# The last three token tiles as a block of two and a block of one, with the second column half's rows put off

## The chip, the cores and the metric

One core of a Trainium2 chip runs the whole program. The metric is the device time of one execution in microseconds (us). The core has TensorE (PE; PEld is its weight load), VectorE (DVE), ScalarE (ACT), GpSimd (POOL) and SyncE (SP), whose queue starts every DMA here.

## The reference

Three layers in a row over 4608 tokens of width 512; the heads' outputs of the first are one token's x.

```python
# attention in chunks of 64 tokens, 8 batches x 8 heads, head size 64
attn = softmax(q_c @ k_c.T / 8);  out = attn @ v_c
# feed-forward, hidden width 2048
g = relu(x @ w_in) ** 2;  x = g @ w_out
# soft MoE: 8 experts x 4 slots, hidden width 1024
logits = x @ phi                              # 4608 x 32
d = softmax(logits over tokens);  slot_input = d.T @ x
slot_out[e] = relu(slot_input[e] @ w1[e]) @ w2[e]
c = softmax(logits over slots);   result = c @ slot_out
```

## The kernel before

The 36 token tiles (128 tokens each) go in blocks of 1, 2, 3, 3, ... tiles, 13 blocks. A block takes 16 steps, one for each 128 of the 2048 hidden units (index f). In a step `moe_h` makes 12 matmuls with the block's x as the moving operand (3 x 128 columns for three tiles) into the PSUM tile hps; ACT applies relu (`moe_relu`) and square (`moe_square`), and two steps later (`LAG`) PE turns the result (`moe_turn`, tile gT) and `moe_keep` copies it into one of seven buffers G, a buffer for every four steps (a quad). After each quad `moe_logits` adds g times w_out times phi to the logits L. x is never multiplied with w_out in full: `soft(b)` folds each block into a running softmax over tokens (Ls, the matmul misc<-Ls,sel, exp, dd) and adds dd times G into a PSUM tile y (L933, 4 quads x tiles matmuls), which DVE adds to `acc`. Only the four G buffers of a block hold what y still needs.

`soft` is a generator: one piece in each step that follows its block. In the last block nothing follows, so its pieces stand one behind the other: L, Ls, softmax, y, acc, then `slot_turn`, `slot_rows_of` (acc times w_out, whose eight buffers are called wo) and `slot_inputs`. What comes out is siT, the input of the experts.

The expert stage reads 33.55 MB of weights: 32 units of w1 and 32 units of w2, each 512 KB (128 partitions x 1024 f32, 4 KB a partition). They have no buffers of their own. `load_units` takes the next unit in a fixed order as soon as two halves (512 f32 each) are free, and starts a DMA on SP's queue: one if the halves lie side by side (L1004), two if not (L1008). `give` at fixed steps puts buffers on that free list: those of attention when the last tiles are done with them, idle G buffers, the input weights wi after their last use (two steps each), x, and after y the last G and wo buffers. In the expert stage a unit's halves are given back as its matmuls are done. SP takes its instructions in order, so a unit that waits for a buffer holds what is behind it.

The expert stage: `ehps` (siT times w1, two groups of four experts), relu, hT by transposes, and `sop` (hT times w2 rows) into two PSUM tiles, one for each half of the 512 columns (ch 0 and 1). Of group 1 the last `FT - SPLIT` row tiles come as units `part`, one for each column half, with rows of 1 KB, so that ch 0 is done first. Then `slot_rows`, `slot_parts` (tile s) and `out_group`: the combine weights cT (made by `c_group`: four transposes and copies for four token tiles) times s, copied from PSUM by ACT and DVE in turn, and stored (9.44 MB in all, 15 stores of 512 KB, 6 of 256 KB). Five output groups of ch 0 alone go ahead, then groups of both halves, then ch 1 of the first five.

On PE the order of the main loop is the order in which the code is written; the other engines' and SP's order is a list scheduler's until the last block's `soft`, from which on ACT and DVE too go as written. `first_use[b]` is the step at which block b starts; attention of its tiles is placed 16 steps and more ahead of that. Before, the last block starts at step u0 = 152.

Of the kernel before, what the change touches and what calls it, by code (L numbers as in the profile page):

```python
# [8 lines left out]
F32 = mybir.dt.float32  # L9
# [7 lines left out]
ALU = mybir.AluOpType  # L17
# [16 lines left out]
C_CHAIN = 0  # L34
C_EARLY = 3
# [39 lines left out]
def kernel(  # L75
# [29 lines left out]
    for n in [1, 2] + [3] * ((NT - 3) // 3):  # L105
        blocks.append((t0, n))
        t0 += n
    if t0 < NT:
        blocks.append((t0, NT - t0))
    NB = len(blocks)  # L110
    bank0 = {1: 1}

    group = {b: b for b in range(NB)}
    blocks.append((0, 3))
    group[NB] = 1

# [18 lines left out]
    run_m = const.tile([P, 1], F32, name="run_m")  # L135
# [234 lines left out]
    def attention(i):  # L370
# [4 lines left out]
        xb = xb_b[max(b, 1) % 2][:, :, :, bank0.get(b, 0) * P :]  # L375
# [191 lines left out]
    def attention32(i):  # L567
# [5 lines left out]
        xb = xb_b[max(b, 1) % 2][:, :, :, bank0.get(b, 0) * P :]  # L573
# [146 lines left out]
    def moe_h(b, f):  # L720
        n = blocks[b][1] * P
        xb = xb_b[max(group[b], 1) % 2][:, :, :, cols(b)]
# [40 lines left out]
    def moe_keep(b, f, eng="act"):  # L763
        k = max(group[b], 1), f // QF
        if k not in G_q:
            G_q[k] = big.tile([P, 3, QF * P], F32, tag=f"G{n_G[0] % NG_RING}", name="G")
            n_G[0] += 1
        o0, n, c = bank0.get(b, 0), blocks[b][1], f % QF * P
        copy(eng, G_q[k][:, o0 : o0 + n, c : c + P], gt_ps.pop((b, f)))
# [18 lines left out]
    def prepare_final():  # L788

        home_ = big.tile([P, 1536], F32, tag=f"xb{NB % 2}", name="siT")  # L790
# [46 lines left out]
    def c_two(x):  # L837

        old, new = (range(max(0, 2 * y), min(C_CHAIN, 2 * y + 2)) for y in (x - 1, x))
        for g in old:  # L840
            c_parts(g, pool)
            if g + 2 < C_CHAIN:
                c_prepare(g + 2)
        for g in new:
            c_transpose(g, ps_h.tile([P, 512], F32, tag="h", name="cps"))
            c_todo.pop(0)
# [3 lines left out]
    def soft(b):  # L850
        s0, n = blocks[NB if b == 1 else b]
        last = s0 + n == NT
        if last:
# [26 lines left out]
        dve.tensor_tensor(out=rm, in0=rm, in1=run_m, op=ALU.max)  # L880
        dve.tensor_scalar_mul(nm, rm, -1.0)
# [3 lines left out]
        act.activation(out=al, in_=run_m, func=ACTF.Exp, bias=nm)  # L885
        if not last:
            dve.tensor_copy(run_m, rm)
# [29 lines left out]
        if not last:  # L917
            slots_softmax(misc()[:, : n * NS])
            yield
# [38 lines left out]
    total_G = NQ * (NB - 1)  # L958
    last_G = [x % NG_RING for x in range(total_G - NQ, total_G)]
# [3 lines left out]
    SPLIT = FT // 4  # L963
# [139 lines left out]
    pool.memset(run_m, -1e30)  # L1103
# [286 lines left out]
    at(u0 - 7, lambda: after_attention(1 - pl))  # L1390
# [5 lines left out]
    at(u0 + 9, lambda: give(*[(big, f"G{x}", 1536) for x in idle_G]))  # L1396
# [7 lines left out]
    while t < end or any(x >= t for x in slots):  # L1404
# [5 lines left out]
        if b is not None:  # L1410
# [3 lines left out]
            if (b, f) == (NB - 1, NF - 1):  # L1414
                give((big, f"xb{b % 2}", 1536))
# [173 lines left out]

    for g in range(2):  # L1590
        for ft in range(SPLIT if g else FT):
            m, t = divmod(ft, 2)
            for ch in range(NCH):
                rows_times(
                    g, ft, ch,
                    lambda ei: part_of(("rows", 4 * g + ei, m), t)[:, ch * DH : (ch + 1) * DH],
                )
            if t:
                for ei in range(4):
                    release(("rows", 4 * g + ei, m), 0)  # L1600
                    release(("rows", 4 * g + ei, m), 1)
                load_units()
# [13 lines left out]
    slot_parts(0, slot_rows(0, sops[0]))  # L1616
    firsts = [quads[0][:2], quads[0][2:], *quads[1:]]
    for ft in range(SPLIT, FT):
        if FT - ft < len(firsts):
            out_group(firsts.pop(0), (0,))  # L1620
        last_rows(1, ft)
# [38 lines left out]
```

## Time and profile before

| | |
|---|---|
| time, median of 3 runs | 762.2 us (761.36 to 765.82) |
| profiled execution: its time, its span | 762.14 us, 760.3 us |
| busy in the span | PE 93%, ACT 60%, PEld 60%, DVE 57%, POOL 21% |
| chain that ended last | PE 72%, DVE 10%, DMA 10%, ACT 2% |
| DMA | 110.48 MB; HBM read 78.71 MB, written 9.44 MB |

Busy shares are means over stages that have different limits, so the stages are read apart: the stretches of 40 slices, the windows and the chain.

### The profile page before, as it was taken

To read this page: it belongs to the slowest core of one execution; us is meant where nothing else is said; L and a number is where in the kernel's file an instruction comes from. 1 tells how busy PE (TensorE), PEld (TensorE's weight loads), DVE (VectorE), ACT (ScalarE), POOL (GpSimd) and SP (SyncE) were. 2 spreads that over 40 slices of the span, in tenths; PEclk is the share of its full clock that TensorE was granted. 3 is DMA by queue.
4 is the path that set the end of the run, shared out by engine and by line. 5 is a ranking of instruction groups with operands and counts; after the bars stand their busy time and mean duration, and the time that the engine had idled before them with its cause. 6 is when DMAs were issued, how large, how long until landed. Compare 5 with 4: busy or idle time off the path is not lost.

```text
span 760.3 us, 16721 instructions
## 1 busy us (share of the span) xinstructions
PE 704.4 (93%) x6644; PEld 455.8 (60%) x6644; DVE 430.2 (57%) x912; ACT 455.0 (60%) x947; POOL 157.2 (21%) x205
## 2 busy tenths in 40 slices
PE   5688999988999999999999999999999999979990
PEld 4577776655656566665665666656656666534550
DVE  4789996367756655566666565566655501012241
ACT  3678887664666666566566666666666555521251
POOL 3223211131222303222232122230322300000100
PEclk9899999999999999999999999999999999999996
DMA  8898834234545455434645455545546832659999
GB/s 157 220 232 214 215 120 139 65 76 84 99 93 122 94 97 97 85 84 92 123 94 107 75 99 105 105 89 105 98 84 126 227 107 84 209 184 393 364 328 322
DMA packets 233359, 110.48 MB, mean 145 GB/s; under 512 B 201537, under 2 KB 219969, under 8 KB 233281
## 3 DMA queue, kind: packets, MB, share of 16 engines
q1 hardware_dynamic: 233280, 109.41, 57.8%
q8 instruction: 53, 0.87, 0.5%
q14 instruction: 26, 0.20, 0.1%
HBM read 78.71 MB, written 9.44 MB: 116 GB/s over the span
## 4 chain that ended last, share of the span: by engine, by line
PE 72%; DVE 10%; DMA 10%; ACT 2%; POOL 1%; issue 1%; SPq 1%; DVEq 0%; POOLq 0%; ACTq 0%
PE hps L727 42%; PE gT L761 7%; PE L L778 4%; PE misc L933 4%; DMA qkT<-qk 2%; PE ehps L1477 2%; DMA unit<-in_moe_w_dram 2%; DVE qk L276 2%; DMA qkv<-in_k_dram 1%; DMA qkv<-in_v_dram 1%; PE sop L1584 1%; DMA pT<-p 1%; DVE o L1546 1%; PE misc L498 1%; DVE qk L275 1%
## 5 line engine op out<-in xcount | busy, mean ns | idle before, releaser
L727 PE MATMUL hps<-xb,wi 128*128 128x384 f16 (+2 forms) x2400 | 407.3, 320 | 0.2
L727 PEld LDWEIGHTS <-wi 128*128 128x128 f16 x2400 | 224.6, 98 | 138.2 <-issue 16.8
L742 ACT ACTIVATE g<-hps,inv_w 128x384 f32<-128x384 f32 (+1 forms) x200 | 112.6, 563 | 111.1 <-PE hps L727 109.1
L182 DVE TENSOR_REDUCE am<-qkv 128x1 bf16<-128x512 f32 x90 | 61.8, 687 | 91.3 <-DMA qkv<-in_v_dram 46.4
L188 ACT ACTIVATE G<-gT 128x384 f32<-128x384 f32 (+1 forms) x200 | 94.1, 471 | 16.9 <-PE gT L761 14.4
L761 PE MATMUL gT<-ident,g 128*128 128x128 f32 x576 | 97.7, 277 | 4.5 <-ACT G L188 3.6
L749 ACT ACTIVATE g<-g 128x384 f32<-128x384 f32 (+2 forms) x188 | 96.8, 515 | 1.5
L761 PEld LDWEIGHTS gT<-ident,g 128*128 128x128 f32 x576 | 72.8, 144 | 29.4 <-ACT g L749 6.9
L420 POOL TENSOR_SCALAR vbd<-qkv,as 64x512 f16<-64x512 f32 x54 | 37.2, 689 | 87.0 <-PE misc L500 71.4
L471 POOL TENSOR_TENSOR ex<-ex,rs 128x512 f32<-128x512 f32 x27 | 29.3, 1083 | 123.2 <-DVE rs L468 117.1
L410 DVE SCALAR_TENSOR_TENSOR qk<-qkv,as,qk 128x512 f16<-128x512 f32 x54 | 39.4, 757 | 22.1 <-ACT qk L405 21.5
L425 DVE SCALAR_TENSOR_TENSOR vbd<-qkv,as,vbd 64x512 f16<-64x512 f32 x54 | 44.5, 824 | 0.7
L778 PE MATMUL L<-g,wp 128*32 128x384 f32 x384 | 41.7, 498 | 0.0
L405 ACT ACTIVATE qk<-qkv,as 128x512 f16<-128x512 f32 x54 | 36.8, 716 | 7.2 <-DVE as L215 7.2
L484 POOL TENSOR_TENSOR p<-ex,p 128x512 f16<-128x512 f32 x27 | 36.2, 1340 | 16.8 <-ACT p L481 16.2
L481 ACT ACTIVATE p<-ex 128x512 f16<-128x512 f32 x27 | 17.0, 629 | 37.1 <-POOL ex L471 37.1
L933 PE MATMUL misc<-G,dd 128*32 128x512 f32 x288 | 35.1, 622 | 0.4 <-DVE rs__8934 L941 0.4
L435 DVE COPY qbd<-qkT 64x1024 f16<-64x1024 f16 x54 | 23.4, 433 | 18.6 <-DMA qkT<-qk 18.0
L510 DVE SCALAR_TENSOR_TENSOR xb<-misc,xb 128x512 f16<-128x512 f32 x27 | 18.5, 684 | 26.5 <-ACT xb L504 26.2
L223 POOL TENSOR_SCALAR iv_all<-ai 128x1 f32<-128x1 f32 x27 | 7.4, 274 | 106.9 <-DVE ai L218 105.9
L461 ACT ACTIVATE ex<-ex,es 128x512 f32<-128x512 f32 x27 | 19.4, 718 | 16.6 <-DVE ex L455 16.5
L859 DVE TENSOR_TENSOR Ls<-L,iv_all 128x384 f32<-128x384 f32 x12 | 6.6, 552 | 39.5 <-PE L L778 39.5
(154 smaller groups left out, 1006.0 us busy)
## 6 DMA issues: line engine op xcount, KB each, us to landing
unit<-in_moe_w_dram SPq DMA_DIRECT2D x38, 512.0 KB, 4.6
unit<-in_moe_w_dram SPq DMA_DIRECT2D x52, 256.0 KB, 5.8
qkv<-in_q_dram SPq DMA_DIRECT2D x72, 128.0 KB, 3.2
qkv<-in_k_dram SPq DMA_DIRECT2D x72, 128.0 KB, 3.5
qkv<-in_v_dram SPq DMA_DIRECT2D x72, 128.0 KB, 3.3
stage<-in_moe_w_in_dram SPq DMA_DIRECT2D x16, 512.0 KB, 5.5
stage<-in_moe_w_out_dram SPq DMA_DIRECT2D x16, 512.0 KB, 6.7
out_dram<-o SPq DMA_DIRECT2D x15, 512.0 KB, 5.5
```

Source lines behind the costliest of these rows:

```text
L182: dve.tensor_reduce(out=am, in_=src, axis=AX.X, op=ALU.max, apply_absolute_value=True)
L188: act.activation(out=out, in_=in_, func=ACTF.Copy)
L405: act.activation(out=qk16[:, 2 * a], in_=flat[:, a], func=ACTF.Copy, scale=v["s"][:, a : a + 1])
L410: dve.scalar_tensor_tensor(out=qk16[:, 2 * a + 1], in0=flat[:, a], scalar=v["s"][:, a : a + 1], in1=qk16[:, 2 * a], op0=ALU.mult, op1=ALU. ...
L420: pool.tensor_scalar(out=dst[0], in0=vin, scalar1=v["s"][pr, 2:3], scalar2=1.0, op0=ALU.mult, op1=ALU.mult,)
L425: dve.scalar_tensor_tensor(out=dst[1], in0=vin, scalar=v["s"][pr, 2:3], in1=dst[0], op0=ALU.mult, op1=ALU.subtract,)
L727: pe.matmul(hp, wi[f][:, wl, kt], xb[:, xl, kt], start=(nm == 0), stop=(nm == 3 * KT - 1))
L742: act.activation(out=g, in_=hp, func=ACTF.Relu, scale=sc)
L749: act.activation(out=g, in_=g, func=ACTF.Square)
L761: pe.transpose(gt_ps[b, f][:, j], g[:, j * P : (j + 1) * P], ident)
L778: pe.matmul(L_ps[g0][NS * x : NS * x + NS, :n], wp[:, QF * q + x], g[:, x, :n], start=(q == 0), stop=(q == NQ - 1), tile_position=(0, NS * x),
L933: pe.matmul(y[NS * g : NS * g + NS], dd[:, j], G_q[b, g][:, j], start=(j == 0), stop=(j == n - 1), tile_position=(0, NS * g), skip_group_c ...
```

## The change

The last three tiles become a block of two (b = 12) and a block of one (b = 13), 14 blocks in all. Block 12 runs in steps 152 to 167, block 13 in steps 168 to 183, and u0 is now 168. The two share one x buffer (`x_of`: tile 35 stands behind tiles 33 and 34). Block 13's quads 0, 1 and 2 are copied into the three thirds of one buffer G (quad 3 has a buffer of its own), and all these copies are made by DVE. `soft(12)` runs beside block 13's steps; its slots softmax comes behind its y.

Buffers are given at other steps. `used_G`, the four G buffers of block 12, are free after y of block 12 (step 176) instead of after the last y. Two of the c transposes and copies (`C_CHAIN`) go into the last block's chain. In the running softmax the negative maximum is kept, which makes of two DVE operations one. In the expert stage 4 row tiles of group 1 instead of 6 come as `part` units (`SPLIT`), and of group 0's row tiles 4 to 7 and group 1's 0 to 3 the ch 1 half is put off (`later`) until ch 0 is done, with output groups between.

```diff
-C_CHAIN = 0
-C_EARLY = 3
+C_CHAIN = 2
+C_EARLY = 5
...
-    for n in [1, 2] + [3] * ((NT - 3) // 3):
+    assert NT % 3 == 0
+    for n in [1, 2] + [3] * (NT // 3 - 2) + [2, 1]:
         blocks.append((t0, n))
         t0 += n
-    if t0 < NT:
-        blocks.append((t0, NT - t0))
     NB = len(blocks)
     bank0 = {1: 1}
+    x_of = {b: (max(b, 1) % 2, bank0.get(b, 0)) for b in range(NB)}
+    x_of[NB - 1] = x_of[NB - 2][0], blocks[NB - 2][1]
...
+        xb = xb_b[x_of[b][0]][:, :, :, o0 : o0 + n]
...
+            if b == NB - 1 and 0 < f // QF < 3:
+                G_q[k] = G_q[b, 0][:, f // QF : f // QF + 1]
+            else:
+                G_q[k] = big.tile([P, 3, QF * P], F32, tag=f"G{n_G[0] % NG_RING}", name="G")
+                n_G[0] += 1
...
-            c_parts(g, pool)
+            c_parts(g, dve)
...
-        dve.tensor_tensor(out=rm, in0=rm, in1=run_m, op=ALU.max)
-        dve.tensor_scalar_mul(nm, rm, -1.0)
+        dve.scalar_tensor_tensor(
+            out=nm, in0=rm, scalar=-1.0, in1=run_n, op0=ALU.mult, op1=ALU.min
+        )
...
+        if short:
+            yield
+        elif not last:
...
+        if short:
+            yield
+            slots_softmax(misc()[:, : n * NS])
...
-    total_G = NQ * (NB - 1)
-    last_G = [x % NG_RING for x in range(total_G - NQ, total_G)]
+    total_G = NQ * (NB - 2)
+    last_G = [x % NG_RING for x in range(total_G, total_G + 2)]
+    used_G = [x % NG_RING for x in range(total_G - NQ, total_G)]
...
-    SPLIT = FT // 4
+    SPLIT = FT // 2
...
-    at(u0 - 7, lambda: after_attention(1 - pl))
+    at(u0 - 12, lambda: after_attention(1 - pl))
...
-    at(u0 + 9, lambda: give(*[(big, f"G{x}", 1536) for x in idle_G]))
+    at(u0 - 5, lambda: give(*[(big, f"G{x}", 1536) for x in idle_G if x not in used_G]))
+    at(u0 + 10, lambda: give(*[(big, f"G{x}", 1536) for x in used_G]))
...
-            moe_keep(b, f)
+            moe_keep(b, f, "dve" if b == NB - 1 else "act")
...
+            now = g == 0 and ft < FT // 2
+            row_tile(g, ft, 0)
+            if now:
+                row_tile(g, ft, 1)
+                if ft % 2:
+                    done_rows(g, ft // 2)
+            else:
+                later.append((g, ft))
             if waiting and ft == 1:
                 hidden_T(*waiting.pop())
-            if c_todo and (t or g):
-                c_group(c_bank(f"ht{ft % 2}" if 1 in hT_g else "ht1"))
+            if c_todo and g == 0 and ft in (3, 5):
...
-    slot_parts(0, slot_rows(0, sops[0]))
+    so_sb = slot_rows(0, sops[0])
     firsts = [quads[0][:2], quads[0][2:], *quads[1:]]
+    for x, (g, ft) in enumerate(later):
+        row_tile(g, ft, 1)
+        if x == 0:
+            slot_parts(0, so_sb)
+        if ft % 2:
+            done_rows(g, ft // 2)
+            out_group(firsts.pop(0), (0,))
+        elif c_todo:
+            c_group(c_bank("ht1"))
+    assert not c_todo
...
-        if FT - ft < len(firsts):
+        last_rows(1, ft)
+        if len(firsts) > 1 and ft >= FT // 2:
             out_group(firsts.pop(0), (0,))
-        last_rows(1, ft)
```

How many units can start by when, counted from the code. Before: 18 by buffers given up to step 159, 5 at step 161 (three idle G, wi4), 6 at steps 163 to 169, so 29; then 6 by the four G after y, 8 by wo, 21 in the expert stage. Now: 1 early, 6 at step 156, 2 at 163 (one idle G), 5 at 167, 4 by wi0 to wi3 up to step 175, so 18; then 1 by wi4 (step 177), 6 by the G buffers of block 12, 6 at steps 179 to 185, so 31; then 3 by block 13's two G, 8 by wo, 22 in the expert stage.

Three places, as the two programs have them. First, PE behind the last step's matmuls: gT is the turn of g, misc is a PSUM bank for L's sums, the turned weights dd and y (<-G,dd), cps are the c transposes.

Before:

```order
L761 MATMUL gT<-ident,g 128x128 x9
L778 MATMUL L<-g,wp 32x384 x4
L869 MATMUL misc<-Ls,sel_68 128x384
L922 MATMUL misc<-ident,dts 128x32 x3
L933 MATMUL misc<-G,dd 32x512 x12
```

Now:

```order
L764 MATMUL gT<-ident,g 128x128 x3
L784 MATMUL L<-g,wp 32x128 x4
L876 MATMUL misc<-Ls,sel_68 128x128
L1069 MATMUL cps<-ident,c_8889 128x2x64 x4
L1069 MATMUL cps<-ident,c_8912 128x2x64 x4
L932 MATMUL misc<-ident,dts 128x32
L943 MATMUL misc<-G,dd 32x512 x4
```

Each piece has a third of the columns or matmuls, and eight c transposes stand between. Second, SP's queue around attention of tile 35, the last one (its qk buffer is qk_81, its pT the last one listed); 128x1024 is a whole unit, 128x512 half of one.

Before:

```order
L1004 DMA unit<-in_moe_w_dram 128x1024 x2
L1008 DMA unit<-in_moe_w_dram 128x512
L487 DMA_TRANSPOSE pT<-p_85 128x8x128
L431 DMA_TRANSPOSE qkT<-qk_81 128x16x128
L1004 DMA unit<-in_moe_w_dram 128x1024 x4
```

Now:

```order
L1018 DMA unit<-in_moe_w_dram 128x1024
L1022 DMA unit<-in_moe_w_dram 128x512
L433 DMA_TRANSPOSE qkT<-qk_81 128x16x128
L1018 DMA unit<-in_moe_w_dram 128x1024
L1022 DMA unit<-in_moe_w_dram 128x512
L1018 DMA unit<-in_moe_w_dram 128x1024 x3
L1022 DMA unit<-in_moe_w_dram 128x512
L489 DMA_TRANSPOSE pT<-p_85 128x8x128
L1022 DMA unit<-in_moe_w_dram 128x512
L1018 DMA unit<-in_moe_w_dram 128x1024
```

Tile 35's two transposes now stand behind more units: 12 and a half are ahead of its pT. Third, PE where ch 0 of the experts' output gets done (sop; four of its rows are one row tile and column half), up to the last s4p.

Before:

```order
L1584 MATMUL sop<-unit,hT 32x256 x24
L1506 MATMUL s4p<-so_sb,sel_68 128x256
L1584 MATMUL sop<-unit,hT 32x256 x8
L1543 MATMUL ops<-s_9375,cT 128x256 x2
L1584 MATMUL sop<-unit,hT 32x256 x4
```

Now:

```order
L1599 MATMUL sop<-unit,hT 32x256 x44
L1521 MATMUL s4p<-so_sb,sel_68 128x256
L1069 MATMUL cps<-ident,c_9654 128x2x64 x4
L1599 MATMUL sop<-unit,hT 32x256 x4
L1558 MATMUL ops<-s_9650,cT 128x256 x2
L1599 MATMUL sop<-unit,hT 32x256 x4
L1069 MATMUL cps<-ident,c_9677 128x2x64 x4
L1599 MATMUL sop<-unit,hT 32x256 x4
```

Behind ch 0 (the first s4p) PE had 6 half row tiles left before; now it has 11 (one more stands just ahead of that s4p) and two c groups.

## Rows read from the trace of the kernel before

**Rows 1.** Page, part 2: 40 equal slices of 19 us; clock in tenths, DMA share.

```profile
PE   5688999988999999999999999999999999979990
PEclk9899999999999999999999999999999999999996
DMA  8898834234545455434645455545546832659999
```

**Rows 2.** Windows: stretch, length, busy us of each engine, PE clock, DMA share, GB/s.

```profile
627.40:654.40 27.00, 27.00 (x191) 15.77 (x193) 4.08 (x14) 14.07 (x32) 0.00 (x0) 1.00 0.34 97
654.40:668.50 14.10, 14.10 (x99) 8.53 (x93) 0.00 (x0) 7.79 (x18) 0.00 (x0) 1.00 0.79 280
668.50:676.50 8.00, 4.43 (x32) 2.25 (x34) 2.12 (x8) 3.16 (x9) 0.00 (x0) 1.00 0.58 202
676.50:682.30 5.80, 4.85 (x28) 1.19 (x20) 0.99 (x2) 0.07 (x1) 0.00 (x0) 0.71 0.08 26
682.30:704.00 21.70, 20.87 (x211) 9.33 (x214) 5.89 (x14) 3.75 (x8) 1.82 (x3) 1.00 1.02 391
712.00:731.80 19.80, 19.14 (x226) 9.43 (x218) 5.33 (x8) 4.95 (x9) 1.85 (x3) 1.00 1.08 346
731.80:744.00 12.20, 10.34 (x72) 8.42 (x71) 10.25 (x17) 10.01 (x18) 0.00 (x0) 1.00 0.95 300
744.00:758.40 14.40, 0.00 (x0) 0.00 (x0) 0.08 (x1) 0.00 (x0) 0.00 (x0) 0.54 1.03 369
```

**Rows 3.** Chain that ended last, in the last block: start us, us, what.

```profile
629.74 0.78 PE L L778 x8
...
632.58 0.33 PE gT L761 x3
632.91 1.95 PE hps L727 x12
634.86 0.65 PE misc L869 x2
...
640.06 0.59 PE misc L901 x6
...
643.85 0.30 PE misc L922 x3
...
648.85 2.71 PE misc L933 x24
```

**Rows 4.** Timeline of PE in the first blocks: one step of one tile, of two tiles.

```profile
49.88 0.83 PE L727 MATMUL hps<-xb,wi 128*128 128x128 f16 x12
54.49 1.47 PE L727 MATMUL hps<-xb,wi 128*128 128x256 f16 x12
```

**Rows 5.** Groups by form on ACT, one tile: busy us, mean ns, idle before.

```profile
L742 ACT ACTIVATE g<-hps,inv_w 128x128 f32<-128x128 f32 x8 | 3.0, 369 | 0.0
L749 ACT ACTIVATE g<-g 128x128 f32<-128x128 f32 x5 | 1.5, 310 | 0.2
```

**Rows 6.** The chain behind the last step: y of the last block, acc.

```profile
667.48 1.96 PE hps L727 x12
...
676.29 4.58 PE misc L933 x24
680.87 0.03 issue
680.90 0.76 DVE acc L944
```

**Rows 7.** The chain at the end of the expert stage.

```profile
715.37 1.86 PE sop L1584 x32
717.23 0.59 PE cps L1055 x4
...
725.51 6.51 DMA unit<-in_moe_w_dram
732.03 0.04 issue
732.07 0.64 PE sop L1584 x8
...
734.96 0.64 PE ops L1543 x3
735.60 0.02 issue
735.62 3.35 DVE o L1546 x6
```

**Rows 8.** Timeline of PE: output groups of ch 0, two and four tiles.

```profile
724.45 0.70 PE L1506 MATMUL s4p<-so_sb,sel 128*128 128x256 f32 x2 [0.56 <-ACT so_sb L1501]
...
726.79 0.50 PE L1543 MATMUL ops<-s,cT 128*128 128x256 f32 x2
...
729.79 0.74 PE L1543 MATMUL ops<-s,cT 128*128 128x256 f32 x4
```

More of the change, by code (lines that the diff above doesn't have):

```diff
@@ L115 @@
     group[NB] = 1
+    x_of[NB] = 1, 0
     const = ctx.enter_context(tc.tile_pool(name="const", bufs=1))
@@ L134 @@
     cmat = None
-    run_m = const.tile([P, 1], F32, name="run_m")
+    run_n = const.tile([P, 1], F32, name="run_n")
     run_s = const.tile([P, 1], F32, name="run_s")
@@ L374, in attention @@
         qk16, ex, p16 = qk16_b[par], ex_b[par], p16_b[par]
-        xb = xb_b[max(b, 1) % 2][:, :, :, bank0.get(b, 0) * P :]
+        xb = xb_b[x_of[b][0]][:, :, :, x_of[b][1] * P :]
         flat = qkv.rearrange("p t c a d -> p t (c a d)")
@@ L572, in attention32 @@
         qkv, ex = qkv_b[par], ex_b[par]
-        xb = xb_b[max(b, 1) % 2][:, :, :, bank0.get(b, 0) * P :]
+        xb = xb_b[x_of[b][0]][:, :, :, x_of[b][1] * P :]
         flat = qkv.rearrange("p t c a d -> p t (c a d)")
@@ L721, in moe_h @@
         n = blocks[b][1] * P
-        xb = xb_b[max(group[b], 1) % 2][:, :, :, cols(b)]
+        o0 = x_of[b][1] * P
+        xb = xb_b[x_of[b][0]][:, :, :, o0 : o0 + n]
         hp = ps_h.tile([P, 512], F32, tag="h", name="hps")[:, :n]
@@ L765, in moe_keep @@
         if k not in G_q:
-            G_q[k] = big.tile([P, 3, QF * P], F32, tag=f"G{n_G[0] % NG_RING}", name="G")
-            n_G[0] += 1
+            if b == NB - 1 and 0 < f // QF < 3:
[3 more added lines that the diff above has]
+                n_G[0] += 1
         o0, n, c = bank0.get(b, 0), blocks[b][1], f % QF * P
@@ L788, in prepare_final @@
     def prepare_final():
-        home_ = big.tile([P, 1536], F32, tag=f"xb{NB % 2}", name="siT")
+        home_ = big.tile([P, 1536], F32, tag=f"xb{1 - x_of[NB - 1][0]}", name="siT")
         n = KT * E * W36
@@ L852, in soft @@
         last = s0 + n == NT
+        short = b == NB - 2
         if last:
@@ L884, in soft @@
         )
-        act.activation(out=al, in_=run_m, func=ACTF.Exp, bias=nm)
+        act.activation(out=al, in_=run_n, func=ACTF.Exp, bias=nm, scale=-1.0)
         if not last:
-            dve.tensor_copy(run_m, rm)
+            dve.tensor_copy(run_n, nm)
         dve.scalar_tensor_tensor(
@@ L916, in soft @@
         yield
-        if not last:
+        if short:
+            yield
+        elif not last:
             slots_softmax(misc()[:, : n * NS])
@@ L1102 @@
     dve.tensor_copy(sel4, sel1.unsqueeze(1).to_broadcast([P, 4, NS]))
-    pool.memset(run_m, -1e30)
+    pool.memset(run_n, 1e30)
     pool.memset(run_s, 0.0)
@@ L1414 @@
             if (b, f) == (NB - 1, NF - 1):
-                give((big, f"xb{b % 2}", 1536))
+                give((big, f"xb{x_of[b][0]}", 1536))
         for fn in slots.pop(t, []):
@@ L1588, in rows_times, with row_tile, done_rows @@
             )
+    later = []
+    def row_tile(g, ft, ch):
+        m, t = divmod(ft, 2)
+        rows_times(
+            g, ft, ch,
+            lambda ei: part_of(("rows", 4 * g + ei, m), t)[:, ch * DH : (ch + 1) * DH],
+        )
+    def done_rows(g, m):
+        for ei in range(4):
+            release(("rows", 4 * g + ei, m), 0)
+            release(("rows", 4 * g + ei, m), 1)
+        load_units()
     for g in range(2):
         for ft in range(SPLIT if g else FT):
[L1592 to L1602, printed above, removed]
+            now = g == 0 and ft < FT // 2
[6 more added lines that the diff above has]
+                later.append((g, ft))
             if waiting and ft == 1:
                 hidden_T(*waiting.pop())
-            if c_todo and (t or g):
-                c_group(c_bank(f"ht{ft % 2}" if 1 in hT_g else "ht1"))
+            if c_todo and g == 0 and ft in (3, 5):
+                c_group(c_bank("ht1"))
     def last_rows(ch, ft):
@@ L1615 @@
         last_rows(0, ft)
-    slot_parts(0, slot_rows(0, sops[0]))
+    so_sb = slot_rows(0, sops[0])
     firsts = [quads[0][:2], quads[0][2:], *quads[1:]]
+    for x, (g, ft) in enumerate(later):
[6 more added lines that the diff above has]
+        elif c_todo:
+            c_group(c_bank("ht1"))
+    assert not c_todo
     for ft in range(SPLIT, FT):
-        if FT - ft < len(firsts):
+        last_rows(1, ft)
+        if len(firsts) > 1 and ft >= FT // 2:
             out_group(firsts.pop(0), (0,))
-        last_rows(1, ft)
     so_sb = slot_rows(1, sops[1])
```

## The prediction

> **What bounds the kernel now.** I read the forty slices first [rows 1]: PE is full from the sixth slice to the thirty-fifth at full clock; from the thirty-seventh the DMA row shows nines almost to the end. So there are two stages with different limits, and the tail has to be read in windows [rows 2]. Up to 668.5 us PE is busy all the time while DMA moves 97 to 280 GB/s, short of free buffers. From 676.5 to 682.3 DMA stands nearly still (share 0.08): the next units wait for the G buffers, which y of the last block still reads; y ends at 680.87 [rows 6]. From 682.3 on the share is about one to the end, at 391 GB/s for weights with long rows, 346 for the `part` units and 300 to 369 for stores. The chain at the end says the same: the ch 1 parts end at 732.03, PE needs 0.64 us for what is left, output groups start at 734.96, and after the copies the stores drain [rows 7].
>
> Hence the reading on which all below rests: **the end is the moment from which the weight queue is never empty again, plus what is then still to be moved, plus what PE needs behind the last weights.** Shortening PE's chain between the last step and the experts helps only if the queue would otherwise stand still.
>
> The profiled execution took 762.14 us, 1.84 more than its span of 760.3, and lies 0.06 under the median of 762.2. I sum against it.
>
> **The change part by part: PE up to the last step.** One step of three tiles takes 1.95 us of matmuls [rows 3]. One of one tile shows 0.83, one of two tiles 1.47 [rows 4]; each holds one drain at its end, so 128 columns cost their difference, 0.64. Split in three by columns, a step costs 1.92; with a drain in each, 2.30. So 16 split steps cost between -0.5 and +5.6 us; I take +0.3, since in the full loop the next matmuls cover the drain.
>
> The same number of turns is made, but block 12's last six now lie ahead of the last step: 6 x 0.11 = +0.65 (0.33 for three, [rows 3]). The logits matmuls take 0.78 a quad for 384 columns; ahead of the last step were three quads (2.34), now there are four of 256 and three of 128. By columns that is 2.86, at full price 5.46; with a small fixed part I estimate 0.57 and 0.35, so +1.0 (ends +0.5 and +3.1). soft(12) is new beside the steps: two thirds of 0.65, of 0.59, of 0.30 and of 2.71 [rows 3], +2.8. Together **+4.8: the last step's matmuls end at 674.2 instead of 669.4** [rows 6].
>
> Beside it: ACT needs 0.37 + 0.31 = 0.68 us for a step of one tile [rows 5], PE 0.64 + 0.11 = 0.75, so ACT just keeps up; the softmax's exponentials can push it behind once, 0 to 1 us, taken as 0. The 16 copies moved to DVE cost nothing: DVE did nothing at all from 654.4 to 668.5 [rows 2]. If that cover were gone, PE would wait for a gT bank. Making one DVE operation out of two in each softmax costs and gives nothing while PE is the bound; in the last chain it gives about 0.16.
>
> **The last chain.** From the last matmul (669.44) to the end of y (680.87) it took 11.4 us, with y at 4.58 for 24 matmuls [rows 6] where 2.71 is the price at full clock [rows 3]. With a third of everything y costs 0.9 to 1.5, and the whole chain some 5.5 to 6 us, so y ends near 680, about one us earlier. The eight c transposes fill a wait for the exponential; their two subtractions stand on DVE ahead of acc and cost up to 0.5. What this is worth depends on the queue.
>
> **The weight queue.** A unit of 524,288 bytes takes 1.34 us at 391 GB/s, a `part` unit 1.52 at 346 [rows 2]. Behind y of block 12 stand seven steps' matmuls (4.5), seven turns (0.8), two logits quads (0.7) and one softmax piece (0.4): it ends 6.4 before 674.2, at 667.8, and step 177 at 668.5. By then buffers for 18 units (and half of a nineteenth) have come free; the last five and a half of them come free in about 654 to 666 and need 7.4 us, so they are in. From 668.5 on the queue has 7 units at once (9 us), 6 more by 675.5 (17 us in all, to 685), 3 from y near 680 (to 689), 8 wo from 685 to 688 (to 700), the others from 688 on. **It never runs dry from 668.5**, with 3 to 5 us in hand. That is earlier than before by 13.8 us, but with 45.5 units to go instead of 35: 10.5 x 1.34 = 14.1. The gain is used up by the later steps at which attention's buffers come free (156 and 167 instead of 145 and 151).
>
> Left are 37.5 units x 1.34 = 50.3 and 8 `part` units x 1.52 = 12.1: ch 0's last part is there at 668.5 + 50.3 + 6.1 = 724.9, the last of all at 730.9. The same prices from 682.3 put the old end at 682.3 + 23 x 1.34 + 12 x 1.52 = 731.3; the row says 732.03, some stores lying between. So the last weights come at about 731.6, **0.4 us earlier than before**: the four `part` units fewer pay for it.
>
> **PE behind ch 0.** Here the change moves work to a worse place. Half a row tile costs 0.465 (1.86 for four, [rows 7]), a c group 0.59 [rows 7], an output group 0.50 or 0.74 [rows 8]. From 724.9: the last part 0.47, eight put-off half tiles 3.72, s4p half of its 0.70 (the rest lies beside them), two c groups 1.18, four groups 2.48, four parts 1.86, together 10.1: 735.0. From there to the groups of both halves took 2.25 (732.71 to 734.96, [rows 7]), so they start at 737.2 instead of 734.96, **+2.3**. The same 7.3 MB are stored behind that. At the least, stores that queue up meanwhile hide it all, and the end moves by the weights' -0.4; at the most it moves by the full 2.3. The nearest row, 300 GB/s from 731.8 to 744 where weights had shown 391 [rows 2], says that the queue waits for output there. I take **+2.1**: a span of 762.4 and a time of 764.2.
>
> **The rivals.**
>
> *Forecast, chance 0.48:* as summed, 764.2. Its own range is 761.5 to 767.
>
> *The stores start early enough, 0.25.* Groups of ch 0 now come while the last weights come in, and nothing is missing from 731.8 to 744. At 369 instead of 300 GB/s those 12.2 us shrink by 2.3; with the weights' 0.4 that gives 759.5, and units landing a few us earlier than I count could make it 756. For it speaks that stretch, against it PE's ten us of work ahead. Below 754.6 (chance 0.10) the queue would need some six units more by 668.5, and the buffers for them are not free.
>
> *The clock falls while PE waits for group 1's weights, 0.20.* Before, PE was busy 4.4 of 8 us from 668.5 to 676.5, and the clock then averaged 0.71 over 5.8 us [rows 2], so half speed (1.2 of 2.4 GHz) for about 3.4. The Trainium skill ("TensorE: Matmul & The Clock Gate", Why this matters for your kernels) says that idle gaps between bursts of matmuls bring the clock to half; the trace agrees with its 0.71. Now PE has no c groups left to fill the stretch from about 713 to 725: eight half tiles, 3.7 of 12 us. Against it: in the old stretch from 712 to 731.8 the clock stayed at 1.00 [rows 2], but PE was busy there. If it falls at 725, 3.4 us at half cost 1.7 (766); if it stays down for all of PE's 10 us, up to 10 more (774). It decides from about 5.6 us: over 769.8. That is the case slower than before by over 1%, about 0.10.
>
> *Narrow matmuls don't pack, 0.03.* If a step of one tile takes the 0.83 us of [rows 4] also in the full loop, because 12 weight loads for 128 columns each can't be covered, block 13 costs 16 x 0.19 = 3.0 us more, 1.9 of it ahead of step 177, and all behind moves: 766. The row itself speaks against it, since it holds a drain. The Trainium skill ("TensorE: Matmul & The Clock Gate", Back-to-back issue gap) states about 81 ns a matmul for a stream of weight loads and 128-column matmuls; twelve of those are 0.97 us, more than the row's 0.83 with its drain, so the trace does not agree, and by that rule it would be 767.5.
>
> *The queue holds up tile 35, 0.04.* The two transposes of tile 35 now stand behind units that wait for buffers; if its x came after step 168, PE would stand still there. Five units between the two transposes are 6.7 us, against seven steps of 1.6 and more. Should it miss, some 4 us: 768.
>
> **How the numbers follow.** A measurement of this kernel tells no difference under about 1%, that is 7.6 us: faster means under 754.6, slower over 769.8. Faster 0.10 is the far end of the second case, slower 0.11 the far end of the clock case and a little of the last, the same 0.79. The range from 757.5 to 769 takes in the forecast, most of the store case, the clock falling once, and the ends of the logits and drain terms where they come ahead of step 177.
>
> **What would show it.** The last step's matmuls should end at 673.5 to 675.5, DMA share near one from about 668 on with no gap like the one at 676.5, y of the last block at 0.9 to 1.5 us, ch 0's last part near 725, the last weights near 731.5, and the first group of both halves between 736 and 738. I am wrong on the queue if its share falls under 0.8 anywhere between 670 and 730, or if weights are all in by 727; wrong on the end if the groups of both halves start before 735; and the clock case is right if the granted clock is under 1.0 between 713 and 737.

## The result, and the profile after

The changed kernel takes **769.0 us** (median of 8 runs, 766.27 to 771.91) against 761.9 for the kernel before beside it: a ratio of 1.0089, 95% interval 1.0066 to 1.0111, about 7 us longer. I had said 764.2, range 757.5 to 769.0, and within 1% as the likeliest: the median lies on the upper end of the range, 4.8 us above my number and outside the 761.5 to 767 that I had given the forecast itself, so a term was mis-sized by about that. The profiled execution took 769.07 us with a span of 767.3.

The rows that answer to [rows 1], of the page's part 2:

```profile
PE   5788999889999999999999999999999999989791
PEclk9899999989999999999999999999999999999996
DMA  7797933234455445554544555453526317599979
```

DMA's nines now begin one slice earlier (the 36th of forty), but the last slice but one shows 7 where a 9 stood: a hole that was not there before. The windows of [rows 2] from 668.5 to 744, same stretches and columns:

```profile
668.50:676.50 8.00, 8.00 (x121) 6.46 (x113) 3.77 (x15) 4.59 (x14) 0.00 (x0) 1.00 0.88 321
676.50:682.30 5.80, 3.39 (x29) 1.71 (x28) 3.69 (x13) 2.01 (x7) 1.20 (x2) 1.00 1.02 379
682.30:704.00 21.70, 20.14 (x186) 9.06 (x190) 6.51 (x16) 3.77 (x8) 1.82 (x3) 0.92 1.03 407
712.00:731.80 19.80, 15.40 (x146) 5.93 (x141) 1.48 (x3) 1.95 (x4) 0.94 (x2) 0.91 1.07 363
731.80:744.00 12.20, 11.33 (x124) 6.79 (x123) 5.96 (x10) 5.41 (x12) 0.29 (x1) 1.00 0.63 213
```

The old gap at 676.5 to 682.3 (share 0.08) is closed, as forecast. In its place the queue now starves from 731.8 to 744: share 0.63 at 213 GB/s, where it had been 0.95 at 300. PE is busy 11.3 of those 12.2 us; DVE and ACT, which make the output, fell from 10 us to under 6.

Why is seen in the chain that ended last, which answers to [rows 7]:

```profile
723.57 5.91 DMA unit<-in_moe_w_dram
...
729.52 0.65 PE sop L1599 x6
...
730.69 0.70 PE s4p L1521 x2
...
738.38 1.86 PE sop L1599 x32
...
742.49 0.64 PE ops L1558 x3
```

Ch 0's last part lands at 729.48. PE then works through the put-off half tiles, the c groups, the first output groups and four parts, and the groups of both halves start at 742.49; before, at 734.96. From there to the end of the span it is 24.8 us, before 25.3.

### The profile page after: what moved, and what is told of

It is laid out like the page before. It is cut to its first block, busy times and chain, and to the rows that moved or that the text cites. A ratio compares the mean times of both kernels' runs of the same rounds, so it can differ in the third digit from the quotient of the medians.

```text
span 767.3 us, 17264 instructions
## 1 busy us (share of the span) xinstructions
PE 711.8 (93%) x6870; PEld 469.6 (61%) x6870; DVE 441.0 (57%) x929; ACT 459.5 (60%) x983; POOL 161.6 (21%) x205
## 3 DMA queue, kind: packets, MB, share of 16 engines
HBM read 78.71 MB, written 9.44 MB: 115 GB/s over the span
## 4 chain that ended last, share of the span: by engine, by line
PE 70%; DMA 12%; DVE 10%; ACT 2%; issue 2%; POOL 1%; SPq 1%; DVEq 0%; POOLq 0%; ACTq 0%
PE hps L730 42%; PE gT L764 8%; DMA unit<-in_moe_w_dram 5%; PE L L784 4%; PE misc L943 4%; DMA qkT<-qk 2%; DVE qk L278 2%; DMA qkv<-in_q_dram 2%; DMA qkv<-in_v_dram 1%; DVE qk L277 1%; DVE stage L283 1%; DMA pT<-p 1%; PE misc L500 1%; PE sop L1599 1%; DVE wo L283 1%
## 5 line engine op out<-in xcount | busy, mean ns | idle before, releaser
L730 PEld LDWEIGHTS <-wi 128*128 128x128 f16 x2592 | 236.5, 98 | 131.0 <-issue 17.8
L745 ACT ACTIVATE g<-hps,inv_w 128x384 f32<-128x384 f32 (+2 forms) x216 | 116.6, 540 | 100.9 <-PE hps L730 98.8
L764 PE MATMUL gT<-ident,g 128*128 128x128 f32 x576 | 101.5, 279 | 5.3 <-ACT G L190 4.9
L190 ACT ACTIVATE G<-gT 128x384 f32<-128x384 f32 (+2 forms) x200 | 92.4, 462 | 16.3 <-PE gT L764 13.6
L752 ACT ACTIVATE g<-g 128x384 f32<-128x384 f32 (+2 forms) x204 | 100.0, 491 | 1.9
L422 POOL TENSOR_SCALAR vbd<-qkv,as 64x512 f16<-64x512 f32 x54 | 39.7, 736 | 99.2 <-PE misc L502 62.0
L784 PE MATMUL L<-g,wp 128*32 128x384 f32 (+2 forms) x416 | 42.5, 473 | 0.0
L225 POOL TENSOR_SCALAR iv_all<-ai 128x1 f32<-128x1 f32 x27 | 9.8, 361 | 92.1 <-DVE ai L220 90.8
L1599 PE MATMUL sop<-unit,hT 128*32 128x256 f32 x256 | 21.8, 402 | 3.8 <-DMA unit<-in_moe_w_dram 3.4
```

Source lines behind the costliest of these rows:

```text
L190: act.activation(out=out, in_=in_, func=ACTF.Copy)
L422: pool.tensor_scalar(out=dst[0], in0=vin, scalar1=v["s"][pr, 2:3], scalar2=1.0, op0=ALU.mult, op1=ALU.mult,)
L730: pe.matmul(hp, wi[f][:, wl, kt], xb[:, xl, kt], start=(nm == 0), stop=(nm == 3 * KT - 1))
L745: act.activation(out=g, in_=hp, func=ACTF.Relu, scale=sc)
L752: act.activation(out=g, in_=g, func=ACTF.Square)
L764: pe.transpose(gt_ps[b, f][:, j], g[:, j * P : (j + 1) * P], ident)
```

## The experiments

The table gives, for each profiled execution, the start of the y at about 505 us (the 24 matmuls misc<-G,dd of one block), of ch 0's s4p and of the first group of both halves, the span, what lies between the last two, and what lies between that y and the end of the span; and, from all runs, the ratio to the kernel before. 0.001 is 0.76 us.

| kernel | y | s4p | both halves | span | between | y to end | ratio, interval |
|---|---|---|---|---|---|---|---|
| before | 505.01 | 724.45 | 734.96 | 760.3 | 25.3 | 255.3 | |
| changed | 505.79 | 730.69 | 742.49 | 767.3 | 24.8 | 261.5 | 1.0089 (1.0066 to 1.0111) |
| e1_no_defer | 504.92 | 729.43 | 739.38 | 764.4 | 25.0 | 259.5 | 1.0046 (1.0028 to 1.0064) |
| e2_defer_only | 507.45 | 731.52 | 744.79 | 769.8 | 25.0 | 262.3 | 1.0095 (1.0061 to 1.0129) |
| e3_blocks_only | 503.76 | 727.09 | 738.01 | 763.1 | 25.1 | 259.4 | 1.0021 (1.0002 to 1.0040) |
| e5_later_between | 505.62 | 731.47 | 739.56 | 765.0 | 25.4 | 259.4 | 1.0063 (1.0042 to 1.0084) |
| e6_blocks_clock | 506.61 | 727.58 | 737.96 | 762.9 | 24.9 | 256.3 | 1.0024 (1.0003 to 1.0046) |
| e7_after_clock | 503.90 | 730.87 | 742.67 | 767.6 | 24.9 | 263.7 | 1.0110 (1.0081 to 1.0138) |
| e8_split_only | 505.20 | 727.15 | 735.62 | 760.7 | 25.1 | 255.5 | 1.0008 (0.9990 to 1.0027) |
| e9_chain_only | 502.48 | 724.62 | 736.49 | 761.4 | 24.9 | 259.0 | 1.0038 (1.0022 to 1.0053) |
| e10_before_clock | 505.33 | 722.94 | 733.41 | 758.8 | 25.4 | 253.5 | 0.9973 (0.9952 to 0.9995) |
| e11_delay_both | 504.04 | 723.36 | 736.57 | 762.1 | 25.5 | 258.1 | 1.0052 (1.0023 to 1.0081) |
| e13_after_split2 | 502.43 | 726.59 | 738.38 | 763.4 | 25.0 | 261.0 | 1.0047 (1.0028 to 1.0065) |

A time in one profile must not be set against another's to the tenth of a us as it stands. The y at about 505 us lies ahead of everything that e2 edits in the kernel before and e13 in the changed one, and yet starts 2.4 us later in the one and 3.4 earlier in the other. Timeline of PE, that y and the last block's, for the kernel before, the changed kernel, e2 and e13 (start, us, what):

```profile
505.01 2.78 PE L933 MATMUL misc<-G,dd 128*32 128x512 f32 x24
...
676.27 4.48 PE L933 MATMUL misc<-G,dd 128*32 128x512 f32 x24 [0.35 <-DVE rs__8934 L941]
```

```profile
505.79 2.78 PE L943 MATMUL misc<-G,dd 128*32 128x512 f32 x24
...
680.53 1.07 PE L943 MATMUL misc<-G,dd 128*32 128x512 f32 x8 [0.57 <-DVE dd L934]
```

```profile
507.45 2.78 PE L933 MATMUL misc<-G,dd 128*32 128x512 f32 x24
...
678.70 4.47 PE L933 MATMUL misc<-G,dd 128*32 128x512 f32 x24 [0.35 <-DVE rs__8934 L941]
```

```profile
502.43 2.78 PE L943 MATMUL misc<-G,dd 128*32 128x512 f32 x24
...
677.17 1.06 PE L943 MATMUL misc<-G,dd 128*32 128x512 f32 x8 [0.57 <-DVE dd L934]
```

From that y to the last one it is 171.26 and 171.25 us in the two programs with the old blocks, 174.74 in both with the new ones: the drift lies ahead of the y, and times counted from it can be compared. Behind the last y single executions still differ. The slots' rows (64 matmuls misc<-wo,yz) take 4.71 us in the changed kernel, 5.35 in e1, 3.66 in e5, 5.01 in e7 and 6.02 in e13, whose programs are alike up to there. So I take durations from profiles and verdicts from the ratios.

**Which part of the change costs the time.** Theory A: the put-off half tiles. Theory B: the split of the last block. The first run takes the put-off away:

```diff
-            row_tile(g, ft, 0)
-            if now: row_tile(g, ft, 1); ...
-            else: later.append((g, ft))
+            for ch in range(NCH):
+                rows_times(g, ft, ch, ...)      # both halves, as before
```

> The changed kernel, with no row tile put off: both column halves of a row tile are multiplied as soon as it is there, and the c groups and output groups stand as in the kernel before (the rows are still split at row tile 4 of group 1). Theory A (the loss is the put-off half tiles: they leave PE idle while group 1's rows come in and stand, about 10 us of work, between ch 0's last part and the groups of both halves): 760 to 763 us, the first group of both halves within 3 us of the last weights as before, and no stretch after 730 us with a DMA share under 0.8. Theory B (the loss is the split of the last block: attention's buffers come free later, so the weights come in later whatever the rows do): 767 to 770 us.

765.75 us: between the two. Half of the loss goes with the put-off tiles, half stays. The reverse, the kernel before with the new expert stage:

```diff
-    SPLIT = FT // 4        # and the old loops
+    SPLIT = FT // 2        # and row_tile, later, done_rows, the new output order
```

> The kernel before, with only the expert stage of the changed one: rows split at row tile 4 of group 1, the second halves of eight row tiles put off behind ch 0, six c groups left for that stage. Theory A (put-off half tiles are the loss): 767 to 771 us, with a starved stretch of the queue (share under 0.8) behind the last weights. Theory B (the split block is the loss): 760 to 763 us.

768.16 us, A's number: on the old blocks this stage costs the whole 7 us alone, by the ratio (7.2) and from the y to the end (262.3 against 255.3). Its window from 731.8 to 744 shows the same hole:

```profile
731.80:744.00 12.20, 12.12 (x125) 6.50 (x124) 6.03 (x9) 5.64 (x11) 1.82 (x3) 1.00 0.53 178
```

The blocks alone, with the old stage:

```diff
-C_CHAIN = 2;  C_EARLY = 5;  SPLIT = FT // 2;  new expert stage
+C_CHAIN = 0;  C_EARLY = 3;  SPLIT = FT // 4;  old expert stage
```

> The changed kernel's blocks, its buffers and its softmax, with the whole expert stage of the kernel before (rows split at row tile 2, nothing put off, no c groups in the last chain). Theory A (put-off half tiles are the loss): 759 to 763 us; the queue is never dry behind 672 us, and the last weights come within 1 us of 732. Theory B (the split block is the loss): 766 to 770 us, with the last weights at 735 or later.

763.75 us, 0.75 above A's range and 2.25 below B's: the split blocks cost about 1.6 us (0.2 to 3.0). The last weights come late, as B had it (its chain of waits at the end):

```profile
735.12 0.64 PE sop L1599 x8
```

735.12 where the kernel before shows 732.07 [rows 7], 4.3 us later when both are counted from the y, and in this execution the end is 4.1 us later too. That is more than the ratio has for the runs, and still not 7 us. Then the number that I had passed over, the row tile from which w2 is split into column halves, alone in the kernel before:

```diff
-    SPLIT = FT // 4
+    SPLIT = FT // 2
```

> The kernel before with one number changed: the rows of w2 are split into column halves from row tile 4 of group 1 instead of 2; nothing is put off. Two more units of weights (2.7 us) then stand ahead of ch 0's last part, and two parts fewer behind it. If ch 0's end sets the time only through the put-off half tiles, 761.5 to 763 us, since the last weights still come near 732; if every us by which ch 0 gets done later is passed on, 764 to 766.

762.99 us, no difference that shows, though ch 0's s4p came 2.5 us later when both are counted from the y, near the 2.7 us of two units. The groups of both halves start only 0.5 us later. And the same number put back in the changed kernel:

```diff
-    SPLIT = FT // 2
+    SPLIT = FT // 4
```

> The changed kernel with one number put back: the rows of w2 are split into column halves from row tile 2 of group 1, as before; six half tiles are put off instead of eight. Two units fewer (2.7 us) stand ahead of ch 0's last part, two parts more behind it. In the kernel before, that number changed nothing (762.99 against 762.50), since PE had slack behind ch 0. If the put-off half tiles have used up that slack, so that each us by which ch 0 gets done earlier counts: 765.5 to 767.5. If the time hangs on the last weights alone: 768.5 to 770.

766.39 us, as expected if slack decides. By the ratios, the split at 4 alone costs 0.6 us on the old blocks (e8) and 0.6 on the new ones (e1 against e9), and with the split at 2 the put-off tiles cost 0.7 (e13 against e9); none of the three is told from none. With the split at 4 the put-off tiles cost 3.3 us on the new blocks (the changed kernel against e1; 1.1 to 5.5) and 6.6 on the old ones (e2 against e8; 3.7 to 9.6). On the new blocks the two together cost 2.6 us more than their sum, between -0.3 and 5.5, so the ratios alone do not settle that they add up to more; the rows point that way. PE had about 10.5 us between ch 0's s4p and the groups of both halves, bound by the last weights. In e8 the split at 4 makes ch 0 late by 2.5 us; two parts fewer behind it (0.93 us) and PE's slack take up all but 0.5. In e2 the groups of both halves start 6.9 us later than in e8, counted from the y, and the put-off work with four c groups is 8 x 0.465 + 4 x 0.59 = 6.1 us: it has nowhere to lie. That the same step costs less on the new blocks has two reasons in the rows. The changed kernel leaves two c groups behind ch 0 where e2 leaves four (1.2 us less). And e1, from which the 3.3 are counted, ran at a lower clock while it was PE that the end waited for: from s4p to the groups of both halves it took 9.95 us, e8 with the same loops 8.47 (e1's window, columns as in [rows 2]):

```profile
730.00:736.00 6.00, 5.01 (x34) 2.43 (x34) 1.81 (x3) 1.58 (x3) 0.00 (x0) 0.72 0.70 233
```

The two c groups in the last chain, on the new blocks and the old stage:

```diff
-C_CHAIN = 0;  C_EARLY = 3
+C_CHAIN = 2;  C_EARLY = 5
```

> The run with the changed blocks and the old expert stage, with the change's two c groups in the last chain (their two subtractions stand on DVE ahead of acc, 1.31 us in the changed kernel) and five instead of three beside the experts' first matmuls. If the 1.3 us ahead of acc are passed on: 764.5 to 766. If the weights set the end there and PE's start does not: 763 to 764.5, as without them.

764.63 us, where the two expectations meet: 0.9 us more than e3 (by the ratios 1.3), with intervals that overlap. It stays open whether this part costs anything.

Last, the put-off tiles moved in among ch 0's parts:

```diff
     for ft in range(SPLIT, FT):
+        for g, r in later[2 * (ft - SPLIT) : 2 * (ft - SPLIT) + 2]:
+            row_tile(g, r, 1)
         last_rows(0, ft)
...
```

(The c groups move with them, and the output groups of ch 0 come to stand among the parts of ch 1.)

> The changed kernel with the put-off second halves moved only: two of the eight stand ahead of each of ch 0's four parts instead of all eight behind the last one. Theory A: the 3.7 us of half tiles and two c groups fill the time in which PE waits for units between 713 and 729 us, so 762 to 764 us; if the lower clock seen at 724 to 728 us comes from PE idling there, the granted clock is 1.00 from 713 to 737. Theory B (the split block is the loss): no change, 767 to 770 us.

766.25 us: by the ratios it gives back 2.0 of 6.8 us (-0.4 to 4.3, so not told from none), less than A had. The clock expectation missed as well (columns as in [rows 2]):

```profile
720.00:724.00 4.00, 2.98 (x20) 1.03 (x20) 0.00 (x0) 0.00 (x0) 0.00 (x0) 0.67 1.03 335
724.00:728.00 4.00, 3.92 (x49) 2.20 (x52) 0.71 (x2) 1.19 (x2) 0.00 (x0) 0.90 1.10 355
```

PE is busy 2.98 of the first four us, where it waits for units; the granted clock averages 0.67 there and 0.90 in the next four, the moved work comes late, and s4p starts no earlier than 731.47.

**Is it the clock?** In the changed kernel the clock fell at 724 to 728, my third case's sign. Five matmuls of no use ahead of each part of ch 0 were to hold it up:

```diff
     for ft in range(SPLIT, FT):
+        fill(c_bank("ht1"), 5)
         last_rows(0, ft)
```

> The changed kernel with five matmuls of no use (128 columns, results never read) on PE ahead of each of ch 0's four parts, where PE waits for units from 713 to 729 us. If the lower clock at 724 to 728 us lengthens the end, the clock stays at 1.00 there and the time falls by 1.5 to 3 us, to about 766 to 767.5. If PE only waits for ch 0's last part there, as the chain of waits says (it lands at 729.5 whatever the clock), the clock stays up and the time does not move: 768 to 770.

769.80 us, no gain. The changed kernel's window with the one behind it, and this run's:

```profile
724.00:728.00 4.00, 3.87 (x21) 0.94 (x20) 0.00 (x0) 0.00 (x0) 0.00 (x0) 0.57 1.10 344
728.00:732.00 4.00, 3.66 (x33) 1.64 (x34) 0.16 (x1) 0.90 (x3) 0.52 (x1) 1.00 1.08 348
```

```profile
724.00:728.00 4.00, 4.00 (x41) 2.85 (x44) 0.00 (x0) 0.00 (x0) 0.00 (x0) 1.00 1.08 348
```

0.57 became 1.00, but this run does not price the clock, because the filling took the place of the wait. Ch 0's last part was issued at 722.2 and in flight 5.9 us, so it was there at 728.1; PE came to it at 729.73, out of its own filling (cps L793, in the chain that ended last):

```profile
728.42 1.31 PE cps L793 x10
729.73 0.61 PE sop L1609 x8
...
730.87 0.70 PE s4p L1531 x2
```

The rows of the changed kernel itself say that the fall at 724 to 728 delayed nothing there: PE waited for the part until 729.48, the clock was back at 1.00 by then, and s4p starts 1.21 us behind the landing, as in e13 (725.38 and 726.59). The same in the last chain of the run with the split blocks:

```diff
+            fill_h(2)   # ahead of the last turn, and 2, 4, 1, 4, 1 in the waits behind it
             moe_turn(b, f)
```

> The run with the changed blocks and the old expert stage, with 14 matmuls of no use in the waits of PE's last chain, where the clock had fallen to half at 678 to 686 us (the 64 matmuls of the slots' rows took 6.06 us instead of 3.78). If the clock is what eats the shorter chain: clock 1.00 there, those 64 matmuls in 3.8 us, the experts start near 686.7 instead of 689.0, and the time is 1.5 to 2.5 us shorter than without the filling, 761 to 762.5. If the weights alone set the end: as without it, 763 to 764.5.

763.78 us, as without it, although the clock did what was asked: by the ratios 0.2 us more than e3, between -2.0 and 2.4. The slots' rows, first of e3, then of this run:

```profile
681.40 5.93 PE L823 MATMUL misc<-wo,yz 128*32 128x256 f32 x64
```

```profile
684.06 3.66 PE L833 MATMUL misc<-wo,yz 128*32 128x256 f32 x64
```

Against this one execution of e3 2.3 us of PE's work are saved, and in this pair the end comes earlier too: from the y to the end it is 256.3 us instead of 259.4. In e3 the chain that ended last runs through these rows and the experts' first matmuls into the queue (SPq), and the queue's share falls where this run's, in the same stretch counted from the y, does not:

```profile
681.40 6.06 PE misc L823 x64
...
701.28 5.41 PE ehps L1492 x48
706.69 0.13 SPq L1022
```

```profile
703.76:708.76 5.00, 5.00 (x64) 2.23 (x57) 0.69 (x1) 0.60 (x1) 0.00 (x0) 1.00 0.80 269
```

```profile
706.61:711.61 5.00, 4.12 (x56) 2.62 (x52) 1.38 (x2) 1.06 (x3) 0.12 (x1) 1.00 1.04 374
```

The clock does not cost the same in every execution (the rows took 3.66 to 6.02 us, above), which may be why the runs show no gain. What it is worth in the last chain of the new blocks stays open. In the kernel before, where the queue stands still for y, the same trick must count:

```diff
+            fill_h(3)   # ahead of the last turn, and 2, 7, 1, 4, 1 in the waits behind it
             moe_turn(b, f)
```

> The kernel before, with 18 matmuls of no use in the waits of PE's last chain. y of the last block (24 matmuls) took 4.58 us there at half clock and takes 2.71 at full clock, and the units that wait for its G buffers come 1.9 us earlier. If the end is the moment from which the queue is never empty again plus what is then to be moved: 759.5 to 760.5 us. If PE's clock there does not pass on: 761.5 to 762.

759.65 us, as expected, and faster than both kernels. Its window that answers to the gap in [rows 2], then its y and its first group of both halves on the timeline:

```profile
676.50:682.30 5.80, 5.71 (x60) 3.00 (x62) 1.67 (x6) 0.38 (x1) 0.00 (x0) 1.00 0.32 95
```

```profile
676.59 2.78 PE L948 MATMUL misc<-G,dd 128*32 128x512 f32 x24
...
733.41 8.12 PE L1562 MATMUL ops<-s,cT 128*128 128x256 f32 x55 [0.87 <-DVE s L1529]
```

y takes 2.78 us, where the same view of the kernel before has 4.48, and the queue's share in the gap rises from 0.08 to 0.32. The rule of the Trainium skill ("TensorE: Matmul & The Clock Gate", Why this matters for your kernels), that gaps between bursts of matmuls bring the clock to half, holds here in reverse: with the gaps filled, the granted clock stayed at 1.00.

**Does the end follow the groups of both halves?** In the kernel before, 13 matmuls of no use stand ahead of them:

```diff
     so_sb = slot_rows(1, sops[1])
+    fill(c_bank("ht1"), 13)
```

> The kernel before, with 13 matmuls of no use (some 0.21 us each, 2.8 us) on PE ahead of the groups of both column halves, so that these start 2.5 to 2.8 us later; the weights and the groups of ch 0 are untouched. If the end follows the start of these groups at a fixed distance (25.3 us in the kernel before, 24.8 in the changed one): 2.4 to 2.9 us longer than before, 764.5 to 765.5. If the queue has stores enough to hide such a delay, as my second case had it: 762 to 763.

764.22 us, 0.3 below the first range and above the second; the ratio says 4.0 us (1.8 to 6.2). Counted from the y, the groups of both halves start 2.6 us later than in the kernel before and the end comes 2.8 later. Nothing is hidden:

```profile
731.50 3.17 PE L787 MATMUL cps<-phi_sb,sel 128*128 128x128 f32 x26
...
736.57 8.13 PE L1553 MATMUL ops<-s,cT 128*128 128x256 f32 x55 [0.87 <-DVE s L1520]
```

## Why the prediction was right or wrong, point by point

**That the range holds the time is luck.** Four of the eight runs lie above 769.0. I had set the range's upper part for the clock falling once and for the ends of the logits and drain terms; none of them made the time longer in the rows. The size of one term was wrong, below.

**PE up to the last step: right in its parts, 2.0 us late in the trace.** I had the last step's matmuls end at 674.2; they end at 676.2. The rows that answer to [rows 3] in block 13, from the chain:

```profile
666.64 0.67 PE hps L730 x12
667.32 1.85 PE misc L943 x16
```

A step of one tile takes 0.67 (I had 0.64), y of two tiles 1.85 (two thirds of 2.71 are 1.81). Of the 2.0 us, 0.8 is the drift ahead of the y (505.79 against 505.01, above); the rest is spread over small terms. The case of matmuls that don't pack is dead: 0.67 for twelve is 56 ns each, weight loads beside them. The Trainium skill ("TensorE: Matmul & The Clock Gate", Back-to-back issue gap) has about 81 ns for that stream; the measurement decides. Tile 35 held up nothing: PE is busy all through 668.5 to 676.5.

**The last chain: its price was right, its start late.** From the last matmul of the last step (676.2) to the end of y (680.53 and 1.07, above) it took 5.4 us, where I had 5.5 to 6. From the rows that answer to [rows 6]:

```profile
680.51 1.31 DVE cT L1083 x2
...
682.50 0.76 DVE acc L954
...
684.52 4.76 PE misc L823 x64
689.29 8.63 DMA unit<-in_moe_w_dram
```

The two c subtractions took 1.31 us ahead of acc and put it off by about 0.8, not 0.5: PE waits 1.71 us for acc there and 0.90 in e3. The slots' rows ran partly at half clock. Whether that reached the end is open: the chain that ended last runs through these rows into the queue, but the transfer behind them was in flight for 8.63 us in a queue that was full (share 1.03 from 682.3 to 704, above).

**The queue: count right, start three us late.** From the windows of the changed kernel:

```profile
668.50:670.50 2.00, 2.00 (x26) 1.36 (x18) 0.95 (x2) 0.36 (x1) 0.00 (x0) 1.00 0.75 205
670.50:672.50 2.00, 2.00 (x36) 1.70 (x35) 1.30 (x7) 1.21 (x5) 0.00 (x0) 1.00 0.76 279
...
668.50:767.30 98.80, 72.87 (x731) 39.45 (x723) 30.33 (x68) 25.93 (x56) 4.25 (x7) 0.90 0.95 342
```

342 GB/s for 98.8 us are 33.8 MB; less 9.44 of output (as before: page, part 3), 24.35 MB or 46.4 units were still to come at 668.5, where I had 45.5. But the share was 0.75 until 672.5, because the step that frees the buffers came later: 0.97 MB in four us instead of 1.54. The two make 1.2 + 1.5 = 2.7 us. In these 2.7 the drift of 0.8 is contained.

**The term that failed: "ch 0's last part is there at 724.9".** It landed at 729.48, 4.6 later, and the end is 4.9 later than summed. 2.7 of it is the queue, above. The other 2 us is in how I counted: as if every byte that comes in belonged to the unit issued first. The window from 672.5 to the landing, the issues on SP's queue in that time, and the issue behind ch 0's last part with its time to landing:

```profile
672.50:729.48 56.98, 48.76 (x490) 22.57 (x488) 14.50 (x38) 11.19 (x28) 3.63 (x6) 0.94 1.04 386
```

```profile
723.57 4.86 SPq L1022 DMA_DIRECT2D unit<-in_moe_w_dram  x7
728.78 0.37 SPq L1018 DMA_DIRECT2D unit<-in_moe_w_dram  x1
```

```profile
L1022 SPq DMA_DIRECT2D unit<-in_moe_w_dram x1: 368/368/368, 724.3 to 724.3; - x1
...
DMA to landing us min/median/max: 5.9/5.9/5.9
```

By 729.48 the queue had moved 386 x 56.98 = 22.0 MB. Everything up to and with ch 0's last part is 24.35 - 0.97 - 4 x 0.524 = 21.28. So 0.7 MB of ch 1's parts had come in ahead of it, 2.1 us at 343 GB/s (the window from 727.4 to 729.5): the half part issued at 723.57 was in flight 5.91 us, and all seven transfers behind it had been issued by then. The Trainium skill ("DMA: Bandwidth & Descriptors", Queues, rings and completion order) says that completion is not in the order of issue for one issuing engine. No row here shows that: the half part issued next, at 724.3, landed at 730.2, 0.7 us behind ch 0's last, and the last 22 transfers of units all landed in the order of their issue. What had come in ahead were bytes of transfers that were not complete yet. I had tested my price on the last unit of all, where that cannot show.

The last weights, issued at 728.78 and in flight 6.5 us, came at 735.3, where I had 731.6. Counted from the y, that is 2.4 us later than in the kernel before, and not 0.4 earlier. In the changed kernel the end does not wait for them, because PE gets to them only behind the put-off work.

**PE behind ch 0: right.** 12.3 us forecast from the last part's landing to the groups of both halves, 13.0 measured; the 0.7 is s4p's wait for so_sb, which I had laid beside other work. So PE's work behind the landing takes what I said, but I had the landing where the old prices put it, and it was the landing that moved.

**The rivals.** My second case, stores that hide PE's work, is refuted: "between" is 24.8 to 25.5 in all thirteen rows of the table, and in e11 a delay is passed on. I gave it 0.25 on the ground that the queue was 0.95 busy from 731.8 to 744; that showed that no store was missing then, not that any was to spare. The clock case had its sign (granted clock under 1.0 from 724 to 728) without its price: PE was waiting for a part there, so the sign should have asked whether PE was the one waited for. e7, meant to test it, cannot, since its filling came to stand in front of the part. Of the signs that I listed, the queue's did fire, for two us: the share is 0.76 in the row from 670.5 to 672.5, and 0.97 or more from there to 732. The first group of both halves, which I wanted between 736 and 738, came at 742.49.

**What is shown and what not.** Shown by runs: the new expert stage on the old blocks makes the whole loss (e2); without putting tiles off, half of it goes (e1), with the split at 2 half of it goes too (e13); the end hangs on the groups of both halves (e11). Read from rows only: the 2.1 us of bytes that came in ahead, and that the clock's fall at 724 to 728 delayed nothing. Open: whether the split at 4 and the put-off tiles together cost more than their sum (2.6 us, -0.3 to 5.5); whether the c groups in the last chain cost anything (e9); what the clock in the last chain costs on the new blocks (e6); and how the 6.6 and 3.3 us of the put-off tiles divide between their own work and the clock that fell in e1. Each is a difference of two or more ratios, and their intervals are 3 to 6 us wide.

## What to carry to other kernels

Work put off behind a milestone is free only while the milestone's follower has slack, and an edit that makes the milestone later takes from the same slack: add up what every edit takes from the same stretch. Where a queue keeps several transfers in flight, forecast a landing as the issue plus the flight time (here 5.9 us): bytes of the transfers behind it come in meanwhile (0.7 MB here), so the bytes ahead of it give a time that is too early. And before a clock that falls is priced, ask who waits: filling PE's gaps gave 2 us where the weight queue waited for PE (e10), and where PE waited for the queue the filling itself came to stand in the way (e7). Last, look for the point up to which two profiles have drifted apart, and count from there.

## What the runs showed of the hardware that was not expected

Matmuls of no use in PE's waits, 18 of 128 columns, held the granted clock at 1.00 where it had averaged 0.71 [rows 2], and made the kernel 0.27% faster (0.05 to 0.48). Without them the same 64 matmuls behind the last y took 3.66 to 6.02 us in five programs that are alike up to there. And profiles of programs that are alike up to there stand up to 3.4 us apart after 500 us (505.79 and 502.43), more than most edits here are worth, while the next 174.74 us agree to the hundredth.
